# Nyström attention with a gated MLP on one core: later requests for q, k and v, the second group's scores behind the first group's transposes, and a pause behind each front

## The chip, the cores and the metric

The kernel runs on one core of a Trainium2 chip. The metric is the device time of one execution in microseconds, from the runs of the kernel; beside it stands one profiled execution, whose trace all rows come from. The engines are called as in the profile: PE multiplies matrices, PEld loads its weights, DVE is the vector engine, ACT the scalar engine, POOL the third elementwise engine, and SP issues all DMAs here. "Clock" is the share of its full clock that PE was granted.

## What is computed

```python
# q, k, v: (8 images, 8 heads, 576, 64) float32
q_lm = q.reshape(B, H, 32, S // 32, D).mean(axis=3)     # 32 landmarks
k_lm = k.reshape(B, H, 32, S // 32, D).mean(axis=3)
A, Bm, C = sm(q, k_lm), sm(q_lm, k_lm), sm(q_lm, k)     # softmax of scaled scores
Z = Bm.T / (norm1(Bm) * norminf(Bm) + 1e-6)
for _ in range(6):
    Z = 2 * Z - Z @ Bm @ Z
x = (A @ Z @ C @ v).transpose(0, 2, 1, 3).reshape(4608, 512)
xn = x / sqrt(mean(x * x) + 1e-6) * rms_g
out = (silu(xn @ w_gate) * (xn @ w_val)) @ w_out        # 512 -> 1536 -> 512
```

## The kernel before

Each image is taken in two groups of four heads, g = 0 and 1. Its attention part is a set of generators. `stage1(b, g)` sums q and k to landmarks (`lmT`, two DVE reductions), then multiplies the scores: this is called the **front** here, sixteen `sC`/`sA` multiplications for each 288 columns and one small one, into four PSUM banks of the pool `pa`, which has four banks in all. The maxima (`mx`), the exponentials `E` and `eb` (ACT) and the transposes `tA` (DVE) empty these banks. Its second half, `back()`, takes the softmax of A (`mA`, POOL's subtraction, ACT's exponential, `sumA`, POOL's product, `AT`), transposes `E` on PE (`sE`, `sF`) and multiplies with v (`pCV`). `newton(b)` runs the iteration (`p`, `pn`, `pW`, `pT`), `second(b)` multiplies the attention output's squares (`pO`, `sq`, `pss`, `pms`), and its end is a chain of small DVE steps `ms`, `r` and then `tA`, `af`, `an`: `an` is the normalized image that the MLP reads, for both groups.

The MLP takes the hidden width in two halves: first all eight images with the first half (`mlp(early, ...)`, chunk 0 to 7, partial sums written to memory), then all eight with the second (`mlp(late, ...)`). A chunk multiplies six tiles of the hidden width (`psg`, `psv` into four banks of the pool `pg`; ACT's Silu and DVE's product free them; `h`), then the outputs (`pso`). Weights are split into a high and a low part, and the gate and value weights are multiplied with the attention factor `WT` first (`pM`, then `Mhi` on ACT and `Mlo` on DVE, from the same `pg` banks). A weight tile is loaded (`fetch`), put together by one ACT and three DVE instructions (`load_next`), in the order of a list.

What orders the two is a `Mixer`: each MLP multiplication adds a planned time (`MMG`, `MMO`) to a clock, and after each one generator whose due time has come is run to its next `yield`. `yield a, w` says that the part takes a of planned PE time and may go on w after it (times `slack`); `yield -w` asks again after w. PE's multiplications keep this program order; other engines' orders come out of a scheduler that moves instructions by readiness and priority, so that the code alone does not show them. Requests for DMAs wait on SP's queue in order, for their buffer to come free too.

Of the kernel before, what the change touches and what calls it, by code (L numbers as in the profile page):

```python
# [12 lines left out]
AF = mybir.ActivationFunctionType  # L13
# [21 lines left out]
BW = 5.0  # L35
SW2 = 2.4
# [5 lines left out]
WW = 1.0  # L42
WAIT0 = 3.0
WAIT1 = 4.0
NPAIR = 3
NF1 = 2 * NPAIR


@with_exitstack
def nystrom_moe_kernel(  # L50
# [12 lines left out]
    nc = tc.nc  # L63
    w_gate, w_val, w_out = (w.bitcast(I32) for w in (w_gate, w_val, w_out))
    B, G = q.shape[:2]
# [55 lines left out]
    class Weights:  # L121
# [28 lines left out]
        def load_next(self):  # L150
            if not self.order:
                return
            f, nm = self.order.pop(0)
            while (f, nm) not in self.raws:
                self.fetch()
            raw, shp = self.raws.pop((f, nm))
            whead, wtail = raw[..., 1], raw[..., 0]
            if nm == "o":
                wf = mp.tile(shp, F32, name="w32", tag="w32", bufs=WB)
            else:  # L160
                pair = f // 2
                if pair not in self.gv:
                    self.gv[pair] = self.place("gv", pair), []
                at = (f % 2 * 2 + "gv".index(nm)) * P
                wf = self.gv[pair][0][:, :, at : at + P]
                self.gv[pair][1].append(nm)
            w = wf.bitcast(I32)
            with tc.issue_after(self.after) if self.after else nullcontext():
                nc.scalar.activation(wf, whead.bitcast(F32), AF.Copy, scale=2.0**-112)
            nc.vector.tensor_scalar(  # L170
                w, w, 3, 1, op0=ALU.logical_shift_left, op1=ALU.bitwise_or
            )
            nc.vector.scalar_tensor_tensor(
                w, whead, -0x80000000, w, op0=ALU.bitwise_and, op1=ALU.bitwise_or
            )
            nc.vector.scalar_tensor_tensor(
                w, wtail, 29, w, op0=ALU.logical_shift_right, op1=ALU.bitwise_or
            )
            if nm == "o":
                hi, lo = self.place("o", f)  # L180
                nc.scalar.copy(hi, wf)
                nc.gpsimd.tensor_sub(lo, wf, hi.bitcast(F32))  # L182
                self.out[f] = hi, lo
            while self.queue and len(self.raws) < self.ahead:
                self.fetch()
# [7 lines left out]
    class Mixer:  # L193

        def __init__(self):
            self.streams = []
            self.clock = 0.0
            self.slack = SLACK0

        def add(self, gen, urgent=False):  # L200
            self.streams.append([gen, 0.0, urgent])

        def part(self):
            for st in list(self.streams):
                if st[1] > self.clock:
                    continue
                with tc.high_priority() if st[2] and HP else nullcontext():
                    wait = next(st[0], None)
                if wait is None:
                    self.streams.remove(st)  # L210
                elif not isinstance(wait, tuple):
                    st[1] = self.clock - wait
                else:
                    self.clock += wait[0]
                    st[1] = self.clock + wait[1] * self.slack
                    return True
            return False
# [6 lines left out]
        def drain(self, done):  # L224
            while self.streams and not done():
                if not self.part() and self.streams:
                    self.clock = max(self.clock, min(st[1] for st in self.streams))

    mix = Mixer()

# [1 line left out]
        fs = range(f0, f0 + NF1)  # L232
        return [(f, nm) for f in fs for nm in "gv"] + [(f, "o") for f in fs]

    mixed, gated = {}, {}

    def mix_weights(wts, b, pair):

# [21 lines left out]
    def mlp(wts, b, f0, an, store, part, following):  # L260
# [4 lines left out]
        for n, pair in enumerate(pairs):  # L265
# [4 lines left out]
            for i in range(2):  # L270
                s = mp.tile([P, S], F32, name="s", tag="s", bufs=2)
                for e in range(2):
                    cols = slice(e * HS, (e + 1) * HS)
                    banks = []
                    for z in range(2):
                        ps = pg.tile([P, 512], F32, name=f"ps{'gv'[z]}", tag="pg")
                        at = slice((2 * i + z) * P, (2 * i + z + 1) * P)
                        for g in range(G):
                            for w, a in ((mhi, 0), (mhi, 1), (mlo, 0)):
                                mm(  # L280
                                    ps[:, :HS],
                                    w[:, g, at],
                                    an[:, a, g, cols],
                                    start=(g == 0 and w is mhi and a == 0),
                                    stop=(g == G - 1 and w is mlo),
                                )
                                yield MMG
                        banks.append(ps[:, :HS])
                    nc.scalar.activation(s[:, cols], banks[0], AF.Silu)  # L289
                    nc.vector.tensor_mul(s[:, cols], s[:, cols], banks[1])  # L290
                if len(hs) < NF1:
                    f = len(hs)
# [37 lines left out]
    with tc.tile_pool(name="ap", bufs=1, side="right") as ap, tc.tile_pool(  # L330
# [19 lines left out]
        def stage1(b, g):  # L350
# [5 lines left out]
            with tc.issue_after(gated[b - 2].ins) if b > 1 else nullcontext():  # L356
                for z in range(2):
# [3 lines left out]
                        axis=AX.X,  # L361
                        op=ALU.add,
                    )
            nxt = (b, 1) if g == 0 else (b + 1, 0)
            if b > 0 and nxt[0] < B:
                load_qk(*nxt)
                load_v(*nxt)
            yield 0.0, KW2
            while b and g and stage["second"] < 0:
                yield -0.3  # L370

            sC = [pa.tile([P, 512], F32, name="sC", tag="pa") for e in range(2)]
            sA = [pa.tile([P, 512], F32, name="sA", tag="pa") for e in range(2)]
# [11 lines left out]
            for h in range(4):  # L385
                mm(
                    psB[rows(rho(g, h)), :],
                    lmT[half(h), 0, h // 2, :],
                    lmT[half(h), 1, h // 2, :],
                    start=True,  # L390
                    stop=True,
                )
            sC = [s[:, :HS] for s in sC]
            sA = [s[:, :HS] for s in sA]
            mx = sm.tile([P, 3], F32, name="mx", tag="mx")
# [22 lines left out]
            for e in range(2):  # L418
# [1 line left out]
                    tA[:, e * (NB // 2) : (e + 1) * (NB // 2), :].rearrange("p n m -> p (n m)"),  # L420
                    sA[e],
                )
            yield 1.3, 0.0
            if g == 1:
                stage["front"] = b

            def back():
                yield -BW * mix.slack
                while b and stage["second"] < 0:
                    yield -0.3  # L430
                mA = sm.tile([P, NB], F32, name="mA", tag="mA")
# [19 lines left out]
                EL = ap.tile([2 * M, P], F32, name="EL", tag="EL", bufs=1)  # L451
                nc.scalar.copy(ET, sE)
                nc.scalar.copy(EL, sF)
                yield 0.65, SW2
                pCV = pa.tile([P, D], F32, name="pCV", tag="pa")
                for ch in range(5):
                    for h in range(4):
# [6 lines left out]
                            stop=(ch == 4),  # L464
                        )
                nc.vector.tensor_scalar_mul(nt["PV"][:, g, M:], pCV, rs[:, 0:1])
                yield 0.85, 0.2
                done[b] = done.get(b, 0) + 1
                if done[b] == 2:
# [158 lines left out]
        nc.sync.dma_start(gsb, rms_g.rearrange("(k p) -> p k", p=P))  # L628
        nc.gpsimd.tensor_scalar_mul(gsb, gsb, RS)

        stage = {"front": -1, "first": -1, "newton": -1, "second": -1, "chunk": -1, "outs": -1, "wt": -1}

        def firsts():
            for b in range(1, B):
# [27 lines left out]
        mix.add(stage1(0, 0))  # L662
        mix.add(stage1(0, 1))
        mix.drain(lambda: False)
        for _ in range(4):
            early.fetch()
        load_qk(1, 0)
        load_v(1, 0)
        for _ in range(4, NF1 + 2):
            early.fetch()  # L670
        early.ahead, early.after = 2, fixed["eb", 0, 0].ins
        mix.add(seconds(), True)
# [23 lines left out]
        def lates():  # L696
            while stage["first"] < B - 1:
# [5 lines left out]
            late.spots = itertools.cycle(  # L703
                [(lq, "lraw", 4), (mp, "wraw", 2), (lq, "lraw", 4)]
            )
            yield from late.stream(WAIT1, 5)
            while "rest" not in places:
                yield -0.3
# [4 lines left out]
        late = Weights(order, place_late, ring, 5)  # L713
# [76 lines left out]
```

## Time and profile before

| | us |
|---|---|
| median of 3 runs | 862.11 (861.26 to 862.2) |
| the profiled execution, whole | 866.44 |
| its span from first to last instruction | 864.6 |
| PE busy | 806.0 |
| DVE busy | 519.2 |
| ACT busy | 326.3 |
| mean clock granted to PE | 0.959 |

The profiled execution was 4.33 us longer than the median of the runs, and 1.84 us of it lie outside the span. Chunk 0 begins its `psg` multiplications in earnest at 63.1 us of the span, chunks 1 to 7 at 133.0, 197.0, 254.2, 318.7, 374.8, 438.9 and 485.8, and the second half of the width at 532.0 us. In rows of a timeline the columns are the start, the length, the engine, the line, the operation with what it writes and reads, and in brackets how long the engine was idle before and what it waited for. In rows of windows, each engine has its busy time and in brackets the number of instructions, then the granted clock and the DMAs' share.

### The profile page before, as it was taken

The page shows a single profiled execution, that of the slowest core. Times are in us where ns is not written, and L with a number is a line of the kernel's source. Part 1 is how long each engine was busy: PE and PEld are TensorE (multiplying, and loading weights), DVE is VectorE, ACT ScalarE, POOL GpSimd, SP SyncE. Part 2 cuts the span into 40 slices and gives each one's busy share as a digit, 9 for nine tenths or more (in the row PEclk, how much of TensorE's full clock was granted, in tenths as well). Part 3 has the DMA queues.
Part 4 walks back from the last instruction along what each step waited for, and adds up shares of the span by engine and source line. Part 5 has one row for each costly group of instructions (what it writes and reads, how often), then busy time and mean ns, then how long its engine had stood idle before and what let it go on. Part 6 is the DMA issues. An engine that isn't in the chain of part 4 may idle for free.

```text
span 864.6 us, 17425 instructions
## 1 busy us (share of the span) xinstructions
PE 806.0 (93%) x7190; PEld 635.9 (74%) x7190; DVE 519.2 (60%) x1131; ACT 326.3 (38%) x708; POOL 82.5 (10%) x109
## 2 busy tenths in 40 slices
PE   6548989989989999899899999999999999999998
PEld 3326757767768678678578697888888888878796
DVE  6998996674765855875975972443334242525341
ACT  3246445344354434343453653232223131404140
POOL 2012320020120110110201030000000000000000
PEclk7578999999989999999999999999999999999999
DMA  9654453151151250430262821123221323131202
GB/s 325 223 205 147 137 176 119 38 205 41 62 180 30 97 185 2 138 131 2 80 208 80 308 81 50 58 95 103 76 92 61 104 74 104 50 128 50 73 25 73
DMA packets 41054, 95.49 MB, mean 110 GB/s; under 512 B 4112, under 2 KB 17424, under 8 KB 38928
## 3 DMA queue, kind: packets, MB, share of 16 engines
q1 hardware_dynamic: 40976, 94.39, 32.0%
q8 instruction: 56, 0.92, 0.5%
q14 instruction: 22, 0.18, 0.1%
HBM read 66.06 MB, written 28.31 MB: 109 GB/s over the span
## 4 chain that ended last, share of the span: by engine, by line
PE 76%; DVE 17%; ACT 3%; DMA 3%; issue 1%; POOL 1%; SPq 0%; DVEq 0%; ACTq 0%; POOLq 0%
PE pso L104 27%; PE psg L104 19%; PE psv L104 18%; PE pM L104 4%; PE pn L104 2%; DVE lmT L358 2%; DVE Mlo L255 1%; PE pO L104 1%; PE pCV L104 1%; DVE mx L399 1%; DVE tA L419 1%; DVE tA L605 1%; DVE an L610 1%; DMA wrawv<-in_moe_w_val_dram 1%; DVE af L608 1%
## 5 line engine op out<-in xcount | busy, mean ns | idle before, releaser
L104 PE MATMUL pso<-whio,h 128*128 128x512 f32 x432 | 147.2, 413 | 2.2 <-ACT ob L683 2.2
L290 DVE TENSOR_TENSOR s<-s,psv 128x288 f32<-128x288 f32 x192 | 86.4, 450 | 85.8 <-PE psv L104 76.9
L104 PE MATMUL pso<-lhio,h 128*128 128x512 f32 x432 | 136.5, 392 | 0.0
L289 ACT ACTIVATE s<-psg 128x288 f32<-128x288 f32 x192 | 78.7, 412 | 99.2 <-PE psg L104 99.0
L298 DVE TENSOR_TENSOR h<-s,h 128x576 fp32r<-128x576 f32 x96 | 72.9, 760 | 56.5 <-ACT h L297 56.5
L104 PEld LDWEIGHTS pso<-whio,h 128*128 128x128 f32 x432 | 84.2, 197 | 26.1 <-ACT ob L683 4.9
L254 ACT CAST Mhi<-pM 128x512 fp32r<-128x512 f32 x96 | 51.5, 590 | 132.1 <-PE pM L104 131.9
L104 PEld LDWEIGHTS pso<-lhio,h 128*128 128x128 f32 x432 | 81.1, 188 | 22.5 <-DVE obl L742 5.9
L297 ACT CAST h<-s 128x576 fp32r<-128x576 f32 x96 | 64.6, 673 | 85.4 <-DVE s L290 85.4
L104 PE MATMUL psg<-an,Mhi 128*128 128x288 f32 x384 | 87.3, 310 | 6.0 <-ACT an L609 4.0
L104 PE MATMUL pso<-wloo,h 128*128 128x512 f32 x216 | 89.7, 415 | 0.5 <-POOL wloo L182 0.5
L742 DVE TENSOR_TENSOR obl<-obl,pso 128x512 f32<-128x512 f32 x36 | 24.6, 687 | 104.3 <-PE pso L104 104.3
L255 DVE TENSOR_TENSOR Mlo<-pM,Mhi 128x512 fp32r<-128x512 f32 x96 | 61.8, 681 | 41.4 <-ACT Mhi L254 41.4
L104 PE MATMUL psv<-an,Mhi 128*128 128x288 f32 x384 | 85.7, 305 | 0.0
L104 PE MATMUL pso<-lloo,h 128*128 128x512 f32 x216 | 84.1, 389 | 0.0
L104 PE MATMUL psg<-anl,Mhi 128*128 128x288 f32 x384 | 81.7, 301 | 0.6 <-DVE Mlo L255 0.6
L104 PE MATMUL psv<-anl,Mhi 128*128 128x288 f32 x384 | 79.1, 294 | 0.0
L104 PEld LDWEIGHTS psg<-an,Mhi 128*128 128x128 f32 x384 | 62.5, 191 | 16.6 <-ACT an L609 4.1
L104 PEld LDWEIGHTS psg<-anl,Mhi 128*128 128x128 f32 x384 | 61.0, 188 | 15.5 <-issue 12.6
L104 PEld LDWEIGHTS psv<-an,Mhi 128*128 128x128 f32 x384 | 63.0, 190 | 4.2 <-issue 2.4
L104 PEld LDWEIGHTS psv<-anl,Mhi 128*128 128x128 f32 x384 | 61.5, 188 | 0.0
L104 PE MATMUL psv<-an,Mlo 128*128 128x288 f32 x192 | 58.5, 304 | 0.0
(136 smaller groups left out, 1262.8 us busy)
## 6 DMA issues: line engine op xcount, KB each, us to landing
qk<-in_q_dram SPq DMA_DIRECT2D x16, 576.0 KB, 5.7
qk<-in_k_dram SPq DMA_DIRECT2D x16, 576.0 KB, 6.7
ad<-an SPq DMA_DIRECT2D x8, 1152.0 KB, 5.1
pd<-ob SPq DMA_DIRECT2D x36, 256.0 KB, 2.7
anl<-ad SPq DMA_DIRECT2D x8, 1152.0 KB, 5.1
obl<-pd SPq DMA_DIRECT2D x36, 256.0 KB, 2.7
out_dram<-obl SPq DMA_DIRECT2D x36, 256.0 KB, 2.0
vt<-in_v_dram SPq DMA_DIRECT2D x16, 512.0 KB, 4.1
```

What stands on the lines that cost most here:

```text
L104: tc.keep_in_program_order(nc.tensor.matmul(*args, **kw))
L254: nc.scalar.copy(hi[:, g], ps[g])
L255: nc.vector.tensor_sub(lo[:, g], ps[g], hi[:, g].bitcast(F32))
L289: nc.scalar.activation(s[:, cols], banks[0], AF.Silu)
L290: nc.vector.tensor_mul(s[:, cols], s[:, cols], banks[1])
L297: nc.scalar.copy(h[:, 0, TAIL:], s)
L298: gated[b] = nc.vector.tensor_sub(h[:, 1, TAIL:], s, h[:, 0, TAIL:].bitcast(F32))
L358: nc.vector.tensor_reduce(lmT[:, z], qk[z].rearrange("p h (m c) -> p h m c", c=LM), axis=AX.X, op=ALU.add,)
L399: nc.vector.tensor_reduce(mx[:, e : e + 1], sC[e], axis=AX.X, op=ALU.max)
L419: nc.vector.transpose(tA[:, e * (NB // 2) : (e + 1) * (NB // 2), :].rearrange("p n m -> p (n m)"), sA[e],)
L605: eng.tensor_mul(tAs[g], tAs[g], r1.unsqueeze(2).broadcast_to([P, NB, M]))
L742: nc.vector.tensor_add(ob, ob, ps)
```

## The change

It has these parts. `load_qk` and `load_v` for image b + 1 are asked for behind the last multiplication that reads the same group of image b (`sC`/`sA` for q and k, `pCV` for v), not at the start of `stage1`; at the beginning both groups of image 1 are asked for between the first weights. The front of group 1 waits until group 0's `ET` and `EL` are written (`stage["turned"]`) and one more us, where it followed group 0's front by its due time alone. Behind each front of images 1 to 7 the mixer runs no generator for 2.0 us of its clock (`QUIET`); the back of group 0 of image 1 loses its first pause. The second half's first five weight tiles are asked for ahead of their stream, and their first ACT step is ordered behind the last Silu issued so far.

```diff
@@ load_next
-            with tc.issue_after(self.after) if self.after else nullcontext():
+            after = self.after or silu.get("last")
+            with tc.issue_after(after) if after else nullcontext():
                 nc.scalar.activation(wf, whead.bitcast(F32), AF.Copy, scale=2.0**-112)
@@ Mixer.part
+            if self.clock < self.quiet:
+                return False
...
                     self.clock += wait[0]
+                    self.quiet = self.clock + sum(wait[2:])
@@ Mixer.drain
-                    self.clock = max(self.clock, min(st[1] for st in self.streams))
+                    self.clock = max(self.clock, self.quiet, min(st[1] for st in self.streams))
@@ mlp
-                    nc.scalar.activation(s[:, cols], banks[0], AF.Silu)
+                    silu["last"] = nc.scalar.activation(s[:, cols], banks[0], AF.Silu).ins
@@ stage1
-            nxt = (b, 1) if g == 0 else (b + 1, 0)
-            if b > 0 and nxt[0] < B:
-                load_qk(*nxt)
-                load_v(*nxt)
             yield 0.0, KW2
-            while b and g and stage["second"] < 0:
+            while b and g and stage["turned"] < b:
                 yield -0.3
+            if b and g:
+                yield 0.0, 1.0
...
+            if 0 < b < B - 1:
+                load_qk(b + 1, g)
...
-            yield 1.3, 0.0
+            yield 1.3, 0.0, QUIET * (b > 0)
@@ back
-                yield -BW * mix.slack
+                if (b, g) != (1, 0):
+                    yield -BW * mix.slack
...
-                yield 0.65, SW2
+                yield 0.65, 0.0
+                if g == 0:
+                    stage["turned"] = b
+                yield 0.0, SW2
...
                 nc.vector.tensor_scalar_mul(nt["PV"][:, g, M:], pCV, rs[:, 0:1])
+                if 0 < b < B - 1:
+                    load_v(b + 1, g)
@@ beginning
-        for _ in range(4):
-            early.fetch()
-        load_qk(1, 0)
-        load_v(1, 0)
-        for _ in range(4, NF1 + 2):
-            early.fetch()
+        for g in range(2):
+            for _ in range(4 - g * 2):
+                early.fetch()
+            load_qk(1, g)
+            load_v(1, g)
+        for _ in range(2):
+            early.fetch()
@@ lates
+            for _ in range(5):
+                late.fetch()
+            yield -WAIT1
             yield from late.stream(WAIT1, 5)
```

At the end of chunk 2 PE has, before the change, the front of group 1 of image 4 (its last row is `sC<-lmT`) and one output multiplication later the transposes of group 0:

```order
L104 MATMUL sA<-qk_2843,lmT 32x288
L104 MATMUL sC<-lmT 32x32 x4
L104 MATMUL pso<-whio_971,h_831 128x512
L107 MATMUL sE<-ident,E 128x128 x4
L107 MATMUL sF<-ident,E 64x128
L104 MATMUL pso<-wloo_972,h_831 128x512
```

and with the change the transposes stand ahead of it, five output multiplications and the `pM` of chunk 3 between them, and the front is followed by the first `psg` of chunk 3:

```order
L108 MATMUL sE<-ident,E 128x128 x4
L108 MATMUL sF<-ident,E 64x128
L105 MATMUL pso<-wloo_1215,h_1240 128x512
L105 MATMUL pso<-whio_1214,h_1240 128x512 x2
...
L105 MATMUL pM<-wgv_433,WT 32x512 x8
...
L105 MATMUL sA<-qk_2290,lmT 32x288
L105 MATMUL sC<-lmT 32x32 x4
L105 MATMUL psg<-an,Mhi 128x288 x2
L105 MATMUL psg<-an,Mlo 128x288
```

So the transposes no longer stand directly behind the front that fills all four banks; the front itself has moved to the chunk's boundary.

ACT, at the same boundary, before the change (the exponentials of group 1's front, `tA` of its back, then the copies and Silu of chunk 3):

```order
L405 ACTIVATE E,ss<-sC,mx 128x288 x2
L409 ACTIVATE eb,ss<-sC,mx 128x32
L434 ACTIVATE tA<-tA 128x576
L683 COPY ob<-pso 128x512 x2
L254 CAST Mhi<-pM 128x512 x2
L289 ACT_TABLE_LOAD
L289 ACTIVATE s<-psg 128x288 x2
```

and with the change:

```order
L260 CAST Mhi<-pM 128x512 x2
L295 ACT_TABLE_LOAD
L295 ACTIVATE s<-psg 128x288
L411 ACT_TABLE_LOAD
L411 ACTIVATE E,ss<-sC,mx 128x288 x2
L415 ACTIVATE eb,ss<-sC,mx 128x32
L295 ACT_TABLE_LOAD
L295 ACTIVATE s<-psg 128x288 x2
L441 ACT_TABLE_LOAD
L441 ACTIVATE tA<-tA 128x576
L303 CAST h_807<-s 128x576
```

The exponentials now stand between the Silus of chunk 3, with a table load at each switch (four more loads at this boundary, four at that of chunks 4 and 5, two in chunk 0: 26 in all, 16 before).

On PE, in chunk 3, the second half of `pO` of image 4 stood, before, among `psg` and `psv`:

```order
L104 MATMUL psv<-an,Mlo 128x288
L104 MATMUL pO<-AT,W 64x288 x8
L104 MATMUL psg<-an,Mhi 128x288 x2
L104 MATMUL psg<-an,Mlo 128x288
L104 MATMUL psv<-an,Mhi 128x288 x2
```

and now stands eight output multiplications and a `pM` behind the front of group 0 of image 5:

```order
L105 MATMUL sC<-lmT 32x32 x4
L105 MATMUL pso<-wloo_1157,h_1162 128x512
...
L105 MATMUL pM<-wgv_406,WT 32x512 x8
L105 MATMUL pO<-AT,W 64x288 x8
L105 MATMUL pso<-whio_932,h_807 128x512
...
L105 MATMUL pss<-sq,ones 32x288 x8
...
L108 MATMUL sE<-ident,E 128x128 x4
...
L105 MATMUL pms<-sqT,sel 128x18
```

With it `pss` and `pms` of the image that the next chunk reads have moved towards that chunk's start.

More of the change, by code (lines that the diff above doesn't have):

```diff
@@ L44 @@
 WAIT1 = 4.0
+QUIET = 2.0
 NPAIR = 3
@@ L197, in __init__ @@
             self.clock = 0.0
+            self.quiet = 0.0
             self.slack = SLACK0
@@ L233, in weight_order @@
         return [(f, nm) for f in fs for nm in "gv"] + [(f, "o") for f in fs]
-    mixed, gated = {}, {}
+    mixed, gated, silu = {}, {}, {}
     def mix_weights(wts, b, pair):
@@ L629, in nystrom_moe_kernel @@
         nc.gpsimd.tensor_scalar_mul(gsb, gsb, RS)
-        stage = {"front": -1, "first": -1, "newton": -1, "second": -1, "chunk": -1, "outs": -1, "wt": -1}
+        stage = {"front": -1, "first": -1, "newton": -1, "second": -1, "chunk": -1, "outs": -1, "wt": -1, "turned": -1}
         def firsts():
```

## Prediction

> **What bounds the kernel now.** I read the page's engine rows first, then the windows of the stages, then PE's waits, then the timeline at the longest of them.
>
> ```profile
> span 864.6 us, 17425 instructions
> PE 806.0 (93%) x7190; PEld 635.9 (74%) x7190; DVE 519.2 (60%) x1131; ACT 326.3 (38%) x708; POOL 82.5 (10%) x109
> ```
>
> ```profile
> 63.13:133.90 70.77, 61.59 (x683) 45.79 (x682) 65.21 (x146) 39.29 (x85) 21.41 (x21) 0.93 0.49 168
> 254.24:317.90 63.66, 60.51 (x665) 45.73 (x661) 41.61 (x101) 27.03 (x61) 6.26 (x5) 0.97 0.31 103
> 529.50:864.60 335.10, 330.57 (x2185) 278.09 (x2184) 130.44 (x228) 92.76 (x193) 7.12 (x24) 1.00 0.22 76
> ```
>
> PE carries the span. The windows (length, then PE, PEld, DVE, ACT, POOL, clock) are chunk 0, chunk 3 and the second half of the width. In chunk 0 DVE is busy 65.2 of 70.8 us and sets the pace with PE; in chunk 3 PE idles 3.2 us and DVE has room; behind 529.5 us the change reaches nothing. PE's waits from 130 to 500 us (total, times, longest):
>
> ```profile
> PE sE L107 <- DVE tA L419: 10.9, 5, 2.8
> PE psg L104 <- ACT s L289: 1.9, 1, 1.9
> PE sF L107 <- DVE sumA L437: 0.7, 2, 0.4
> PE sF L107 <- ACT ET L452: 0.7, 1, 0.7
> PE sF L107 <- DVE mx L402: 0.4, 1, 0.4
> ```
>
> `sE` waits once in each of chunks 1 to 5. The timeline at the one of chunk 3:
>
> ```profile
> 299.76 0.26 PE L104 MATMUL sC<-lmT 64*32 64x32 f32 x8
> 299.95 0.51 PE L104 MATMUL pso<-whio,h 128*128 128x512 f32 x1
> 302.36 0.45 DVE L399 TENSOR_REDUCE mx<-sC 128x1 f32<-128x288 f32 x1
> 302.72 0.47 DVE L419 STREAM_TRANSPOSE tA<-sA 128x288 f32<-128x288 f32 x1
> 303.25 0.66 PE L107 MATMUL sE<-ident,E 128*128 128x128 f32 x4 [2.79 <-DVE tA L419]
> ```
>
> Group 1's front has filled all four `pa` banks, and one multiplication later PE stands at `sE` until DVE, busy with `an` and `sumA` until then, has transposed a bank free. The granted clock drops behind each of the five; the windows of the third one, and the sum over all five:
>
> ```profile
> 304.76:308.17 3.41, 3.41 (x10) 2.62 (x9) 2.78 (x7) 1.83 (x8) 2.27 (x2) 0.50 0.91 309
> sum 20.48, PE 18.70 PEld 14.85 DVE 15.88 ACT 11.25 POOL 10.60; mean PE 3.74 PEld 2.97 DVE 3.18 ACT 2.25 POOL 2.12
> ```
>
> **What goes.** The transposes now stand ahead of group 1's front, so these five waits have lost their cause: 10.9 + 0.7 + 0.7 + 0.4 = 12.7 us. For the clock, the starts of output multiplications at full and at half:
>
> ```profile
> 237.10 0.63 PE L104 MATMUL pso<-whio,h 128*128 128x512 f32 x2
> 237.79 0.62 PE L104 MATMUL pso<-whio,h 128*128 128x512 f32 x2
> 245.62 1.05 PE L104 MATMUL pso<-whio,h 128*128 128x512 f32 x2
> 246.90 0.63 PE L104 MATMUL pso<-whio,h 128*128 128x512 f32 x1
> ```
>
> Three take 237.79 - 237.10 = 0.69 us, or 0.23 each; at half clock 1.28 us, or 0.43. Of the 18.70 us worked at half clock 46% is lost, 8.6 us. Together 21.3 us, if no wait takes their place.
>
> The Trainium skill ("TensorE: Matmul & The Clock Gate", Part 1) has the clock drop after at least one idle window of some 3.4 us. The trace disagrees: an idle of 2.79 us within 3.8 us brought 3.41 us at 0.50. By the page the new waits below would cost no clock at all, 1.6 us less than my sum.
>
> **What comes.** Two kinds of wait, both at boundaries of chunks.
>
> First, `an`. Between `pms` and the next chunk's first `psg` now stand, in PE's order, at the ends of chunks 2 and 4, 27 output multiplications, `sE` and `sF`, a `pM` and the front. The `pM` row is:
>
> ```profile
> 437.00 1.09 PE L104 MATMUL pM<-wgv,WT 64*32 64x512 f32 x16
> ```
>
> So 27 x 0.23 + 0.66 + 0.27 + 1.09 + 1.2 (front, an estimate from 16 pairs that end at 300.02 and begin about 298.8) = 9.4 us. At the ends of chunks 3 and 5 the same count gives 9.2 us, of chunk 0 7.6 us, of chunk 1 14 us. Before, this was 25 us and more (`pms` 288.47, chunk 4 from 318.7). DVE's chain from `pms` to the last `an`, undisturbed in chunk 6 and among a front's steps in chunk 3:
>
> ```profile
> 467.87 0.29 PE L104 MATMUL pms<-sqT,sel 128*128 128x18 f32 x2
> 475.86 0.76 DVE L610 TENSOR_TENSOR an<-af,an 128x576 fp32r<-128x576 f32 x1 [0.74 <-ACT an L609]
> 288.47 0.29 PE L104 MATMUL pms<-sqT,sel 128*128 128x18 f32 x2
> 300.29 0.75 DVE L610 TENSOR_TENSOR an<-af,an 128x576 fp32r<-128x576 f32 x1
> ```
>
> 8.5 us from `pms`' end, and 12.3 us. At the ends of chunks 2 and 4 DVE has two `Mlo`, `sumA` and `AT` between the steps, so I take 11.0; group 1's part of `an` is needed 0.5 us after the first `psg`, which leaves a wait of 1.1 us there (0 to 2.4). Chunks 3 and 5 have group 1's maxima in it but neither of these: 9.4 us, no wait (0 to 2.6). Chunk 0: 1.5 us (0 to 4.2). Chunk 1: none.
>
> Second, ACT. Table loads and their cost:
>
> ```profile
> L289 ACT ACT_TABLE_LOAD x8 | 10.3, 1283 | 1.2 <-PE psg L104 1.0
> L405 ACT ACT_TABLE_LOAD x6 | 7.7, 1283 | 22.4 <-DVE mx L402 22.3
> ```
>
> At the starts of chunks 3 and 5 the first Silus stand apart by two loads each time, and the exponentials wait for DVE's maxima in ACT's order. The four added loads take 5.1 us of ACT; the `pg` banks let PE run one half (about 1.8 us) ahead. Followed bank by bank this leaves PE waits of 0.8 and 1.8 us, 2.6 in all per start (0, if the banks cover it, to 5.1). At the starts of chunks 4 and 6, and of chunk 2, the exponentials come ahead of one load, and `Mhi` and Silu come late: 1.3, 1.3 and 0.8 us.
>
> In chunks 3 and 5 the second `pO` stands 8 x 0.23 + 1.09 = 2.9 us behind group 0's front and needs its banks. The front's chain in chunk 3 of before:
>
> ```profile
> 291.22 0.46 DVE L399 TENSOR_REDUCE mx<-sC 128x1 f32<-128x288 f32 x1
> 294.06 0.15 DVE L402 TENSOR_TENSOR mx<-mx,nscale 128x2 f32<-128x2 f32 x1
> 294.14 1.28 ACT L405 ACT_TABLE_LOAD   x1
> 295.44 0.50 ACT L405 ACTIVATE E<-sC,mx 128x288 f32<-128x288 f32 x1
> ```
>
> The first maximum starts about its own length ahead of the front's end, so the factor (294.21) is there 2.5 us behind that end; ACT's load, 1.28 us, then held the exponentials, of 0.5 us each. Without it the second bank is free at about 3.6 us, a wait of 0.7 in each of the two chunks (2.0 with the load as here).
>
> Sum: 1.1 x 2 + 1.5 + 2.6 x 2 + 1.3 x 2 + 0.8 + 0.7 x 2 = 13.7 us. Such short waits can leave the clock alone, as one of 1.91 us in chunk 7 (its row is below) did:
>
> ```profile
> 485.77:529.50 43.73, 41.82 (x266) 36.31 (x263) 27.74 (x48) 19.34 (x38) 6.79 (x5) 1.00 0.42 151
> ```
>
> For one of the two long boundaries I add a slow window, 3.41 x 0.46 = 1.6: 15.3 us.
>
> **The rest.** In chunk 0, before, DVE put together a weight of the second half in the middle of its busiest stretch:
>
> ```profile
> 109.98 0.41 DVE L170 TENSOR_SCALAR w<-w 128x512 int32<-128x512 int32 x1
> 110.43 0.69 DVE L173 SCALAR_TENSOR_TENSOR w<-wrawo,w 128x512 int32<-128x512 int32 x1
> 111.16 0.69 DVE L176 SCALAR_TENSOR_TENSOR w<-wrawo,w 128x512 int32<-128x512 int32 x1
> ```
>
> Its first step is now tied to a Silu, so 1.8 us leave chunk 0, and group 1's `sumA` and `AT` leave it too. I take 2.0 us (0, if PE's order binds, to 4). The one wait on ACT of chunk 7:
>
> ```profile
> 487.53 0.67 ACT L169 ACTIVATE lgv<-wrawv 128x512 f32<-128x512 f32 x1 [1.45 <-DMA wrawv<-in_moe_w_val_dram]
> 489.53 0.53 PE L104 MATMUL psg<-an,Mhi 128*128 128x288 f32 x2 [1.91 <-ACT s L289]
> ```
>
> A late weight held ACT ahead of `Mhi` and Silu. Five weights are now asked for earlier, and their first step goes behind a Silu: 1.9 us go (0 if the loads still come late). The requests for q, k and v:
>
> ```profile
> qk<-in_q_dram SPq DMA_DIRECT2D x16, 576.0 KB, 5.7
> ```
>
> They land within 5.7 us and are needed a chunk (57 to 64 us) later: nothing, though the writes of `ob` and `an` stand in other places behind them on SP; if that cover is gone, a late `qk` holds `lmT` and a front for 5.7 us. The pause adds no instruction; what it delays is `second`, priced above as late `pms`.
>
> In all -21.3 + 15.3 - 2.0 - 1.9 = -9.9 us. The profiled execution took 866.44 us (864.6 span and 1.84 around), so 856.5; it stood 4.33 above the median of 862.11, which gives 852.2.
>
> **Rivals.** (1) The waits move by less: if the banks cover ACT's loads and DVE's chain is near 8.5 us, half of the 15.3 stays, and the time is 844.5. For it speak DVE's 41.6 busy of 63.7 us in chunk 3; against it the in-order ACT at the boundary.
>
> (2) Slower: `an` decides. If its chain takes 12.3 us behind each late `pms`, PE waits 12.3 - 7.6 at chunk 0's end and 2.4, 2.6, 2.4, 2.6 at the next ones, 14.7 us, and each is long enough for a slow window, 5 x 1.6; with 10.0 of ACT's and `pO`'s waits this is 32.7 for 15.3: 869.6. It decides from 25.2 us of new waits on, 5 a boundary.
>
> (3) No change: the new waits just make up 25.2 us, 862.
>
> (4) ACT's order at the two starts costs all that it can: eight added loads of 1.28 us, none covered, are 10.3 us in place of 5.2, and each start gets a slow window, 3.2 us for 1.6: 858.9. Against it speak the `pg` banks, one half ahead.
>
> The Trainium skill ("ScalarE: Activation LUTs", What ACT_TABLE_LOAD costs) speaks harder against the change: a load of about 1.28 us and a drain of some 1.38 at every switch, by which 8 x 2.66 = 21.3 us in place of 5.2 would give 868. The first part agrees with the rows; of the drain they show nothing, since the exponential begins 0.02 us behind its load.
>
> **Numbers.** My forecast 0.45 (its own range 847 to 858), (1) 0.18, (2) 0.20, (3) 0.10, (4) 0.07. The range, 842 to 867, leaves out the worse half of (2) and the case of (1) in which hardly a wait stays. 0.2% (1.7 us) is about what a measurement can tell from no change: faster 0.70 (the forecast, (1) and (4)), same 0.10, slower 0.20.
>
> **What would show it.** `sE <- tA` gone from PE's waits and the clock at 1.00 through chunks 1 to 5: right. New rows `psg <- ACT s` or `psg <- DVE an` at 254, 319, 375 and 439 us less the gain, above 5 us each with slow windows: wrong, rival (2). `pO <- ACT eb` above 2 us: the front's chain was underrated. Chunk 0 no shorter than 70 us: PE's order binds there.

## The result, and the profile after

The changed kernel takes 875.61 us (median of 4 runs, 874.31 to 875.95) against 862.15 for the kernel before in the same session (861.26 to 864.56): ratio 1.0149, 95% interval 1.0126 to 1.0172. It is 13.5 us slower; 852.2 was forecast, with a range that ended at 867. The page's first rows:

```profile
span 873.7 us, 17413 instructions
PE 810.6 (93%) x7190; PEld 638.6 (73%) x7190; DVE 516.3 (59%) x1131; ACT 337.5 (39%) x718; POOL 85.8 (10%) x109
```

The same 7190 multiplications keep PE busy 4.6 us longer, and ACT has ten instructions more, all table loads. Where the time lies is seen in windows from chunk start to chunk start (length; busy time of PE, PEld, DVE, ACT, POOL; clock). Before, chunk 0 and chunks 1 to 7:

```profile
56.50:132.97 76.47, 62.23 (x681) 46.10 (x681) 70.94 (x159) 40.22 (x87) 21.41 (x21) 0.89 0.49 168
132.97:531.99 399.02, 382.12 (x3883) 293.35 (x3875) 270.94 (x630) 175.95 (x385) 46.51 (x50) 0.97 0.32 108
```

and after:

```profile
57.55:138.95 81.40, 65.89 (x695) 47.45 (x695) 63.42 (x145) 39.56 (x82) 18.63 (x19) 0.86 0.46 150
138.95:540.99 402.04, 383.01 (x3904) 295.01 (x3896) 274.91 (x643) 187.03 (x398) 51.03 (x52) 0.98 0.33 111
```

The work ahead of chunk 0 grew by 1.0 us, chunk 0 by 4.9, chunks 1 to 7, which were to gain, by 3.0; the second half of the width is equal to 0.1 us. The trace of before is long for its kernel, though, by 4.3 us. Against the trace of e3 below, whose PE has the same work in the same order and whose two stretches take 75.24 and 394.73 us, chunk 0 grew by 6.2 us and chunks 1 to 7 by 7.3. Note DVE in chunk 0: it worked 71 of 76 us before and only 63 of 81 after. The stretch has become longer and DVE idler, so something else holds it.

**Chunks 1 to 7.** PE's waits after, from 130 to 500 us:

```profile
PE psg L105 <- DVE Mlo L261: 10.4, 4, 2.8
PE psg L105 <- ACT s L295: 4.3, 4, 1.7
PE psg L105 <- DVE an L622: 0.8, 2, 0.4
```

The rows of `sE` and `sF`, 12.7 us together, are gone, and 15.5 us stand in their place. The largest, at the start of chunk 4, on ACT, DVE and PE:

```profile
321.24 1.08 ACT L260 CAST Mhi<-pM 128x512 fp32r<-128x512 f32 x2
322.41 0.26 DVE L511 STREAM_TRANSPOSE nsbt<-nsb 128x128 f32<-128x128 f32 x1
323.83 0.78 DVE L449 STREAM_TRANSPOSE AT<-tA 128x576 f32<-128x576 f32 x1
324.57 0.68 DVE L261 TENSOR_TENSOR Mlo<-pM,Mhi 128x512 fp32r<-128x512 f32 x1
325.24 0.67 DVE L261 TENSOR_TENSOR Mlo<-pM,Mhi 128x512 fp32r<-128x512 f32 x1
325.30 0.54 PE L105 MATMUL psg<-an,Mhi 128*128 128x288 f32 x2 [2.85 <-DVE Mlo L261]
```

`Mhi` is written at 322.3, but on DVE two chains of short steps come ahead of `Mlo`: the start of Newton's iteration (`nsum` to `nden`) and group 1's `sumA` to `AT`. The first output bank of `pM` is thus released at 325.2, and PE stands. In the kernel before neither chain stood ahead of `Mlo` at this boundary, and it was DVE that waited there:

```profile
318.63 1.29 DVE L255 TENSOR_TENSOR Mlo<-pM,Mhi 128x512 fp32r<-128x512 f32 x2 [3.69 <-ACT Mhi L254]
```

So DVE's steps behind a front are the same as ever, and PE waits for them at another place.

A smaller one hides in PE's busy time. In chunk 3 the second `pO` behind group 0's front:

```profile
298.85 1.28 ACT L411 ACT_TABLE_LOAD   x1
299.84 0.71 PE L105 MATMUL pO<-AT,W 32*64 32x288 f32 x8
300.63 0.49 ACT L411 ACTIVATE E<-sC,mx 128x288 f32<-128x288 f32 x1
300.79 1.46 PE L105 MATMUL pO<-AT,W 32*64 32x288 f32 x8 [0.24 <-ACT E L411]
```

The sixteen rows end 2.4 us after they begin, where 0.74 us is usual; only 0.24 us is shown as a wait, since the second bank's wait lies inside the row of 1.46. Chunks 3 and 5 lose 1.7 us each, and chunk 0 2.2.

**Chunk 0.** DVE after, at its start, with group 0's back of image 1 (`mA`, `sumA`, `AT`) and the first steps of the next weights:

```profile
52.73 0.74 DVE L439 TENSOR_REDUCE mA<-tA 128x18 f32<-128x576 f32 x1
56.52 0.73 DVE L443 TENSOR_REDUCE sumA<-tA 128x18 f32<-128x576 f32 x1
61.64 0.77 DVE L449 STREAM_TRANSPOSE AT<-tA 128x576 f32<-128x576 f32 x1
62.97 0.68 DVE L175 SCALAR_TENSOR_TENSOR wgv<-wrawg,wgv 128x512 int32<-128x512 int32 x1
```

Before, the same weight step stood ahead of the back:

```profile
56.25 0.67 DVE L173 SCALAR_TENSOR_TENSOR wgv<-wrawg,wgv 128x512 int32<-128x512 int32 x1
62.39 0.71 DVE L432 TENSOR_REDUCE mA<-tA 128x18 f32<-128x576 f32 x1
```

6.7 us later on DVE: the steps of the back take 2.6 us of it, and two `Mlo` and the end of `an`, which stood behind the weight before, most of the rest. That is not caught up, since the last step on a raw weight frees the buffer that the next request waits for. SP's requests after, in this place (start, length, what):

```profile
64.88 0.38 SPq L148 DMA_DIRECT2D wrawg<-in_moe_w_gate_dram  x1
67.14 0.33 SPq L347 DMA_DIRECT2D qk<-in_q_dram  x1
70.90 0.54 SPq L148 DMA_DIRECT2D wrawv<-in_moe_w_val_dram  x1
```

Before, the two weights were asked for at 58.26 and 67.65. PE, after:

```profile
80.24 1.96 PE L105 MATMUL pM<-wgv,WT 64*32 64x512 f32 x16 [7.95 <-DVE wgv L178]
87.63 0.61 PE L105 MATMUL psg<-an,Mhi 128*128 128x288 f32 x1 [3.10 <-DVE Mlo L261]
```

The second `pM` waits 8.0 us (3.92 before), and the next `psg` another 3.1, for ACT, which copies `Mhi` only when the following weight has landed. The clock is at half for longer: 0.86 over the chunk, 0.89 before.

These waits are not the whole of the 4.9 us. Before, PE had a wait in chunk 0 of the kind that the change removes:

```profile
62.18 1.09 PE L107 MATMUL sE<-ident,E 128*128 128x128 f32 x4 [5.07 <-DVE mx L402]
```

It is gone after, so that PE's idle time in chunk 0 grew only from 14.2 to 15.5 us. The other 3.7 us lie in PE's busy time: 15.7 us were worked at half clock for 10.7 before, the second `pO` hides 1.0 of its 2.2, and the 40 multiplications of group 1's front, done ahead of chunk 0 before (from 51.3 us, where PE then still waited 3.95 for `an`), now stand in it at 65.4.

### The profile page after: what moved, and what is told of

It reads as the page before. It is cut to its first block, busy times and chain, and to the rows that moved or that the text cites. A ratio compares the mean times of both kernels' runs of the same rounds, so it can differ in the third digit from the quotient of the medians.

```text
span 873.7 us, 17413 instructions
## 1 busy us (share of the span) xinstructions
PE 810.6 (93%) x7190; PEld 638.6 (73%) x7190; DVE 516.3 (59%) x1131; ACT 337.5 (39%) x718; POOL 85.8 (10%) x109
## 4 chain that ended last, share of the span: by engine, by line
PE 71%; DVE 17%; ACT 7%; issue 2%; DMA 2%; POOL 1%; SPq 0%; DVEq 0%; ACTq 0%; POOLq 0%
PE pso L105 26%; PE psg L105 17%; PE psv L105 16%; PE pM L105 3%; PE pn L105 2%; PE pO L105 1%; DVE Mlo L261 1%; DVE an L622 1%; DMA qk<-in_q_dram 1%; ACT E L411 1%; DVE af L620 1%; ACT L411 1%; PE sC L105 1%; DVE lmT L364 1%; DVE sumA L443 1%
## 5 line engine op out<-in xcount | busy, mean ns | idle before, releaser
L105 PE MATMUL pso<-whio,h 128*128 128x512 f32 x432 | 142.2, 400 | 0.9 <-DVE h L304 0.9
L105 PE MATMUL psg<-an,Mhi 128*128 128x288 f32 x384 | 93.0, 324 | 25.8 <-DVE Mlo L261 13.5
L105 PEld LDWEIGHTS pso<-whio,h 128*128 128x128 f32 x432 | 80.1, 188 | 24.9 <-issue 6.2
L105 PEld LDWEIGHTS psg<-an,Mhi 128*128 128x128 f32 x384 | 65.5, 200 | 43.2 <-DVE Mlo L261 14.6
L105 PE MATMUL psv<-an,Mhi 128*128 128x288 f32 x384 | 89.2, 314 | 0.5 <-DVE Mlo L261 0.4
L105 PE MATMUL pso<-wloo,h 128*128 128x512 f32 x216 | 86.0, 398 | 0.0
L105 PEld LDWEIGHTS psg<-anl,Mhi 128*128 128x128 f32 x384 | 61.0, 188 | 15.5 <-issue 12.6
L105 PEld LDWEIGHTS psv<-an,Mhi 128*128 128x128 f32 x384 | 65.2, 197 | 5.0 <-DVE Mlo L261 0.9
L105 PE MATMUL psg<-an,Mlo 128*128 128x288 f32 x192 | 60.4, 314 | 0.0
```

What stands on the lines that cost most here:

```text
L105: tc.keep_in_program_order(nc.tensor.matmul(*args, **kw))
```

## The experiments

Each edit is against the kernel named in its diff's first line. "Chunk 0" is the length from its first `psg` to that of chunk 1; ratios are to the kernel before, on the same chip. Lengths of stages come from one trace each, and two traces of one order of work, before and e3, differ by 1.2 us in chunk 0 and by 4.3 in chunks 1 to 7.

### The parts alone

**e1**, the turn alone:

```diff
 # kernel before
-            while b and g and stage["second"] < 0:
+            while b and g and stage["turned"] < b:
                 yield -0.3
+            if b and g:
+                yield 0.0, 1.0
...
-                yield 0.65, SW2
+                yield 0.65, 0.0
+                if g == 0:
+                    stage["turned"] = b
+                yield 0.0, SW2
```

> The kernel before with one part of the change alone: group 1's front waits until group 0's ET and EL are written, and one us more; requests, pause, weights as before. Theory A (the turn is a gain, the pause and what it moves to the chunk boundaries is the loss): the five waits on tA (12.7 us) and most of the half-clock loss behind them (8.6 us) go, with under 6 us of new waits: 842 to 852 us. Theory B (the turn itself makes the second half of the attention late, whatever the pause does; the boundary waits on Mlo and Silu, 14.7 us in the changed kernel, are its price): those waits are there too, 858 to 868 us. Theory C (the loss sits in the beginning, where weights come late): as A, since the beginning is as before.

872.36 us, ratio 1.0109 (1.0059 to 1.0158). No theory foresaw it. PE's waits from 130 to 500 us:

```profile
PE pCV L104 <- DVE tA L421: 10.8, 6, 2.1
PE psg L104 <- DVE Mlo L255: 3.7, 3, 1.8
```

Without the pause `pCV` of group 0 stands one multiplication behind group 1's front, needs one of the four `pa` banks and waits for DVE's `tA` as `sE` did: 10.8 us for 12.7. And chunk 0 is 84.2 us long.

**e2**, the pause alone (`QUIET`, as in the change, on the kernel before):

> The kernel before with the pause of 2.0 us of the mixer's clock behind each front alone. Theory A: the transposes still stand behind group 1's front, so the five waits on tA stay or shrink a little, and the pause moves later parts towards the boundaries: 862 to 870 us, with new psg waits on Mlo or Silu. Theories B and C: the pause alone does nothing that can be measured, 860 to 864 us.

874.91 us, ratio 1.0137 (1.0091 to 1.0182), above all that was expected. Chunk 0 is 81.2 us: the pause alone moves group 1's front of image 1 into it, to 63.2 us, with group 0's transposes still behind that front, at 67.0. Later the wait is `sF` for `mx`, 8.3 us in 5.

**e3**, the requests for q, k and v alone (those of `stage1`, `back` and the beginning):

> The kernel before with the requests for q, k and v alone moved: behind the last use, and at the beginning both groups of image 1 between the first weights. Theory C (late weights at the beginning): the pM of the first pair that waited 3.9 us now waits 6 us or more, and the whole is 866 to 870 us. Theories A and B: the transfers stay hidden, 861 to 864 us.

862.84 us, ratio 1.0007 (0.9978 to 1.0036): no change, chunk 0 75.2 us. On their own the requests are hidden; Theory C falls.

**e4**, the change without its pause:

```diff
 # changed kernel
-QUIET = 2.0
+QUIET = 0.0
```

> The changed kernel with the pause set to 0. Theory A: group 1's fronts leave the chunk boundaries, the psg waits on Mlo (10.4 us from 130 us on) and Silu (4.3) fall below 5 us together and the second pO no longer waits for the exponentials: 855 to 862 us, the rest of the loss being the beginning's. Theory B: the waits stay, 872 to 877 us. Theory C: the beginning is hardly touched by the pause, 868 to 874 us.

866.01 us, ratio 1.0026 (0.9999 to 1.0054), between the ranges of A and C. Mlo's and Silu's waits fall to 2.4 and 0.5 us, but `pCV`'s are 10.2, and chunk 0 is 80.8. Its chunks 1 to 7:

```profile
138.14:531.54 393.40, 377.00 (x3903) 290.51 (x3895) 272.28 (x642) 177.17 (x389) 48.98 (x52) 0.99 0.33 112
```

With the same multiplications on PE they took 402.04 in the changed kernel. The pause thus costs 8.6 us there and hardly anything in chunk 0 (0.6), and the whole is 9.6 us shorter without it. What the four have in common: each one that moves group 1's front of image 1 into chunk 0 (e1, e2 and e4) has a chunk 0 of 81 to 84 us.

### Is it chunk 0?

**e5**, the change, with image 1 in the order of before:

```diff
 # changed kernel
-            while b and g and stage["turned"] < b:
+            while b and g and stage["second" if b == 1 else "turned"] < b - (b == 1):
                 yield -0.3
-            if b and g:
+            if b > 1 and g:
...
-            yield 1.3, 0.0, QUIET * (b > 0)
+            yield 1.3, 0.0, QUIET * (b > 1)
...
-                if (b, g) != (1, 0):
-                    yield -BW * mix.slack
+                yield -BW * mix.slack
```

> The changed kernel, but image 1 (whose attention lies in chunk 0) keeps the order of before: group 1's front ahead of group 0's transposes, no pause, the first pause of group 0's back restored. Theory D (a loss of its own sits in chunk 0, 81.4 us long against 75.2 to 76.5, because group 0's back now enters DVE ahead of the second pair's weights): chunk 0 is 75 to 77 us and the whole 868 to 872 us. Rival E (chunk 0 only hands its work on: what it saves there the later chunks lose): 874 to 877 us.

858.19 us, ratio 0.9944 (0.9921 to 0.9967): 17.4 us less than the changed kernel, and faster than before. Its windows of chunk 0 and of chunks 1 to 7:

```profile
56.69:125.08 68.39, 58.28 (x619) 43.43 (x620) 61.26 (x138) 37.16 (x76) 18.89 (x19) 0.91 0.46 152
125.08:524.79 399.71, 383.15 (x3943) 292.22 (x3935) 277.86 (x651) 179.50 (x395) 51.03 (x52) 0.99 0.34 114
```

Chunk 0 lost 13.0 us, but it also has 76 multiplications fewer, above all the 40 of group 1's front, again ahead of it, and 40 of a `pCV`, now in a later chunk. Chunks 1 to 7 nevertheless lost 2.3 us with 39 more in them, so that the work was not merely handed on: Rival E falls, Theory D holds, and is larger than expected. The boundary waits on `Mlo` and at `pO` are still there; those on Silu fell from 4.3 to 0.5, with 16 table loads as before for 26:

```profile
PE psg L105 <- DVE Mlo L261: 10.4, 6, 2.1
PE pO L105 <- ACT E L411: 3.4, 3, 1.1
```

**e6**, the pause behind group 1's fronts only (`QUIET * (b > 0) * g` in the changed kernel):

> The changed kernel with the pause behind group 1's fronts only, so that the front of group 1 is ten output multiplications and more ahead of the chunk's end and pCV nine behind the front. Theory F (the boundary waits come of the pause behind group 0's front, which pushes group 1's front to the boundary and the second pO behind a front; the waits of pCV without a pause come of its place one multiplication behind the front): psg waits on Mlo and Silu under 4 us from 130 us on (14.7 in the changed kernel), pCV's under 1 (9 without a pause), 858 to 864 us, the rest being chunk 0's. Rival G (a pause anywhere costs): 870 to 876 us.

873.96 us, ratio 1.014 (1.0111 to 1.017). Theory F falls. `pCV` waits only 0.6 us, as expected, but `psg` and `psv` wait for `Mlo` 10.1 us and for ACT's `ob` 3.7, and chunk 0 is 84.5.

**e7**, e5 and e6 together (`QUIET * (b > 1) * g` in e5):

> The two last edits together: image 1 as before, and the pause behind group 1's fronts only. Theories D and F: 850 to 857 us, faster than before. If only F holds, 858 to 864; if only D, 868 to 872.

861.95 us, ratio 0.9981 (0.9961 to 1.0001), 12.0 below e6 by image 1's order alone; chunk 0 is 71.6. Against e5 it gained nothing. It lies in the range given for F alone, but e6 has shown F false: the ranges did not foresee how much image 1's order is worth.

**e8**, the kernel before with e3's requests, and from image 2 on group 1's front behind group 0's `pCV`:

```diff
 # kernel before, with e3's edit
-            while b and g and stage["second"] < 0:
+            while b and g and stage["second" if b == 1 else "turned"] < b - (b == 1):
                 yield -0.3
...
+                if g == 0:
+                    stage["turned"] = b
                 yield 0.85, 0.2
```

> The kernel before with the requests moved, and from image 2 on group 1's front behind group 0's pCV (not only behind its transposes), without a pause: no part that needs a pa bank stands directly behind a front. Theory F (a part that needs a pa bank within a few multiplications of a front waits for DVE; nothing else is lost): no waits of sE, sF or pCV, 850 to 857 us. Rival H (the front stands 5 to 8 output multiplications ahead of the boundary in chunks 2 and 4, and near there its steps hold Mlo and Silu): psg waits of 2 us and more at these boundaries, 860 to 868 us.

859.77 us, ratio 0.9971 (0.9946 to 0.9995). `sE`, `sF` and `pCV` wait no more, and 5.4 us of `Mlo`, 3.2 of `ob` (of `psg` and `psv`) and 1.6 of `sA` for `PV` stand there instead: Rival H, nearly. PE idles 12.9 us in chunks 1 to 7 (16.9 before), and the clock falls in none of its windows from 82 us to 840; but this trace lies 2.3 us below the kernel's median.

### What holds chunk 0

**e9**, a third raw buffer, the order of PE's 7190 multiplications unchanged:

```diff
 # changed kernel
-        ring = itertools.repeat((mp, "wraw", 2))
+        ring = itertools.repeat((mp, "wraw", 3))
...
-        early.ahead, early.after = 2, fixed["eb", 0, 0].ins
+        early.ahead, early.after = 3, fixed["eb", 0, 0].ins
...
-                [(lq, "lraw", 4), (mp, "wraw", 2), (lq, "lraw", 4)]
+                [(lq, "lraw", 4), (mp, "wraw", 3), (lq, "lraw", 4)]
...
-TAB = 5
-ATB = 5
+TAB = 4
+ATB = 4
```

> The changed kernel with a third buffer for raw weight tiles (three may be asked for ahead); the room comes from one buffer less of tA and of AT. PE's order is that of the changed kernel. Theory K (chunk 0 is paced by a chain from weight to weight: DVE's last step on one tile frees its buffer, then request, landing, ACT, DVE; the back of group 0, now ahead on DVE, sits in that chain): the second pair's pM waits under 4 us (8.0 in the changed kernel), chunk 0 falls from 81.4 to 72 to 77 us, the whole is 864 to 871 us. Rival L (DVE's work or PE's order alone sets chunk 0): 79 to 83 us, 873 to 878 us.

869.61 us, ratio 1.0075 (1.0045 to 1.0104), 6.0 below the changed kernel. Chunk 0 and the second `pM`:

```profile
57.37:132.86 75.49, 64.59 (x694) 45.92 (x694) 63.67 (x145) 38.66 (x81) 20.00 (x19) 0.89 0.47 161
77.93 1.96 PE L105 MATMUL pM<-wgv,WT 64*32 64x512 f32 x16 [5.58 <-DVE nden L519]
```

Chunk 0 falls by 5.9 us, and the wait of 3.1 us behind the `pM` falls to 0.3, with the same multiplications in the same order and the same work on DVE. So a chain of requests did hold it in the changed kernel: Theory K. The `pM`'s own wait only fell to 5.6, not below 4, and ends with a step of Newton's start on DVE (`nden`).

**e10**, the turn for image 1 alone:

```diff
 # kernel before, with e1's edit to back()
-            while b and g and stage["second"] < 0:
+            while b and g and stage["second"] < 0 or b == 1 and g and stage["turned"] < b:
                 yield -0.3
+            if b == 1 and g:
+                yield 0.0, 1.0
```

> The kernel before with the turn for image 1 alone: only there group 1's front waits for group 0's transposes, and one us. Theory D (the loss is chunk 0's): chunk 0 is 80 to 85 us against 75.2 to 76.5, later chunks as before, 869 to 874 us, as much as the turn for all images cost. Rival M (the loss of the turn is spread over all chunks): 863 to 866 us.

869.37 us, ratio 1.0082 (1.0052 to 1.0111). Chunk 0:

```profile
55.90:139.25 83.35, 69.01 (x720) 49.98 (x720) 70.60 (x164) 43.72 (x87) 22.23 (x21) 0.84 0.47 155
```

One image's order, in one chunk, costs 7 us, and of PE's work only the 40 multiplications of group 1's front have changed stage, from ahead of chunk 0 into it. The second `pM` waits 6.0 us there. But it begins 20.7 us behind the chunk's start, 19.9 before, both its weights were asked for no later than before (57.6 and 63.4 us for 58.3 and 67.6), and PE's idle time in chunk 0 is the same, 14.3 us for 14.2. The loss lies behind this `pM` and in PE's busy time, with 18.1 us worked at half clock for 10.7. The late requests of the changed kernel are thus not the cause here.

**e13**, the requests back where they were, in the changed kernel (e3 undone):

> The changed kernel with the requests for q, k and v where they were before (at the start of stage1, and at the beginning only group 0 of image 1 between the weights). PE's order is that of the changed kernel. Theory N (the requests stand ahead of the second pair's value weight on SP and share its transfer: 3.3 us of its lateness): the wait at the second pM falls from 8.0 to about 5 us and the whole to 870 to 873 us. Rival O (the requests are hidden): 874.5 to 877 us.

874.75 us, ratio 1.0123 (1.009 to 1.0156). The wait at the `pM` falls by 1.2 us only (6.8), the time by 0.9, which is within the intervals. Theory N is mostly wrong: what delays the second weight is less the requests on SP than the step on DVE that frees its buffer.

**e14**, the first pause of group 0's back restored (`yield -BW * mix.slack` without its condition, in the changed kernel):

> The changed kernel with the first pause of group 0's back in image 1 restored; its transposes then stand 19 multiplications into chunk 0, still ahead of group 1's front. Theory P (the lost pause put the back's DVE steps ahead of the weights'): the wait at the second pM falls below 5 us, 868 to 871 us. Rival Q (the turn does it, wherever the back starts): 873 to 877 us, with a wait of 6 us or more.

872.73 us, ratio 1.0101 (1.0063 to 1.0139). The `pM` waits 5.5 us, less than the 6.0 with the turn alone, but then the first `psg` of chunk 1 waits 7.2 for `an`, and chunk 0 is 86.8: between the two theories.

### Faster ones

**e11**, e5 with the third buffer of e9:

> The changed kernel with image 1's order of before (the kernel of 858 us), and a third buffer for raw weights, with one buffer less of tA and AT. Theory K: chunk 0 falls below 68.4 us, by up to the 3.9 us that its second pM waits, 853 to 857 us. Rival L: the same chunk 0, 857 to 860 us.

856.55 us, ratio 0.9935 (0.9913 to 0.9958). Chunk 0 is 67.2 for 68.4, and its second `pM` still waits 4.0: with the weights' steps early on DVE the third buffer has little left to do.

**e12**, e8's order with the changed kernel's late weights (fetched ahead, first step behind the last Silu):

> The kernel with group 1's front behind pCV from image 2 on, no pause, image 1 as before, and with it the changed kernel's late weights (asked for ahead, first step behind the last Silu). If the late weights' three DVE steps, out of chunk 0, are what shortened it there: chunk 0 is 69 to 72 us (74.9 without), and the whole 853 to 858 us. If it was the pause that shortened it (parts moved into the next chunk): 74 to 76 us, 858 to 861 us.

856.37 us, ratio 0.9924 (0.9897 to 0.9951), with e11 the fastest. Chunk 0 is 72.4 for e8's 74.9: the late weights' DVE steps out of it are worth some 2.5 us, by one trace of each.

**e15**, e12 with the third buffer:

> The fastest kernel so far (group 1's front behind pCV from image 2 on, late weights, image 1 as before) with the third weight buffer, and one buffer less of tA and AT. If the chain of weights still paces its chunk 0 (its second pM waits 3.4 us): 853 to 855.5 us. If not, as without it, 855.5 to 858 us.

857.16 us, ratio 0.9921 (0.9893 to 0.9948): the same as e12. The two do not add up.

## Why the prediction was wrong

Forecast were -9.9 us on the profiled execution; from profile to profile the span grew 9.1. Step by step:

- **The five waits go**: right. 12.7 us of `sE` and `sF` are gone.
- **New waits at the boundaries**, 13.7 us without the clock: the kind was right, the owner partly wrong. `an` was 0.8 us at the boundaries and none at chunk 0's end (forecast 2.2 and 1.5); ACT's order 4.3 (5.2); the second `pO` 1.7 in chunks 3 and 5 (0.7), because the table load that I took for gone was there. The late `Mhi` and Silu at the starts of chunks 2, 4 and 6, 3.4 in the sum, became `Mlo`, 10.4, with a wait of 1.85 us at chunk 1 too. This is one step that failed: I followed ACT's copy and let DVE's `Mlo` come right behind it; DVE's steps of the back and of Newton's start move to this place with the front, and I did not lay them in DVE's row. Together 18.9 for 13.7: these waits alone exceed those that went. The pause brought them, where the prediction let it delay `second` alone. Without it, in e4, `pCV` waits 10.2 us instead, and chunks 1 to 7 are still 8.6 us shorter, by the clock in part (6.8 us worked at half for 12.9).
- **Chunk 0**, -2.0: this is the step that failed most, with 4.9 us the other way. I read DVE's 92% as "DVE sets the pace" and subtracted what left DVE. What came in was not costed: the 40 multiplications of group 1's front, more time at half clock, and group 0's back ahead of the weights on DVE. The window that I read began at 63.13 us, just behind the wait of 5.07 at `sE` that the turn removes, so that the steps not costed are worth more than the 4.9 us show. The subtracted part fits e12's 2.5. The sign named for a mistake here, a chunk 0 no shorter than 70 us, came true, but not its reading that PE's order binds: e9 took 5.9 us off with the same order.
- **The clock**, -8.6 and +1.6: in the trace before, 18.7 us were worked at half clock behind 130 us, after it 12.86, by this row, the sum of the four windows:

```profile
sum 13.65, PE 12.86 PEld 12.65 DVE 6.77 ACT 3.57 POOL 0.27; mean PE 3.21 PEld 3.16 DVE 1.69 ACT 0.89 POOL 0.07
```

  So 5.8 us of work, or 2.7 us of time by the same 46%, came back where 7.0 were counted on: four of the new waits of 1.7 to 2.85 us brought a slow window each.
- **Chunk 7**, -1.9: 0.5 the other way, by its length (46.7 us for 46.2). The wait for Silu is 0.45 instead of 1.91, but 0.94 for `h` has come at the outputs.
- **From the profile to the median**, -4.33: wrong in kind. The excess of the profiled execution was carried over as if the changed kernel had it too; its profile lies at its median. The excess is the clock's: e3's trace has the same waits as before and three slow windows behind 130 us where the trace of before has six, 10.2 us for 20.5. The forecast took these windows off twice, in the 8.6 and in the 4.33.

Added up, the steps miss by 5.2 (waits), 6.9 (chunk 0), 4.3 (clock), 2.4 (chunk 7) and 4.3 (median); with 1.0 us ahead of chunk 0 and 1.0 of `pCV`'s short waits, that is 25.1 for the 23.4 between 852.2 and 875.6, since waits of before on `ob` went as well.

Of the rivals, (2) had the sign, but its mechanism, `an`, made only 0.8 us of wait at the boundaries. The table loads of (4), and the drain that the Trainium skill adds to them ("ScalarE: Activation LUTs", What ACT_TABLE_LOAD costs), did not decide either: e6 has 18 loads where the changed kernel has 26, and is only 1.7 us faster.

What the runs do not settle: why chunk 0 is longer in every order with group 1's front of image 1 inside it. In the eight of these with two raw buffers (the changed kernel, e1, e2, e4, e6, e10, e13, e14) it takes 80.8 to 86.8 us, and in all eight kernels with that front ahead of it 67.2 to 76.5; the turn alone (e10) and the pause alone (e2) are each enough. In the changed kernel e9 shows that the chain of raw buffers carries 5.9 us. In e1, e2, e10 and e14 the weights are asked for as early as before, so that something else, of the clock in part, must hold there. Nor does a run take e5 without any pause, which cost 8.6 us with the other order of image 1.

## What to carry to other kernels

When four banks and one in-order engine stand behind a stretch of work, moving the waiting instruction need not remove the wait: PE stood at `sE`, or at `pCV`, or for `Mlo`, 10 to 13 us in all. Ask which steps must be done, and where nobody waits for them.

A high busy share does not make an engine the bound. In chunk 0 a chain ran through it (last step on a weight, buffer free, request, landing, ACT, DVE), and steps put ahead of a link delay all that follows, though the engine's total work stays the same. Look at what each link waits for before subtracting work.

A gain in one part can hide behind a loss in another: nearly all of the change was kept in e5, and it was faster than before. And a window that begins behind a wait hides what its removal will do. Reading each stage's length first would have shown it at once.

## What the runs showed of the hardware

The granted clock is set in steps of 3.41 us, at places that shift against the program from run to run, and PE's idle time within one step mostly decides the next. The same wait of 2.25 us before `sE` in chunk 2 fell differently in two traces. In the trace of before, one step has 1.51 us of idle time, and half clock follows:

```profile
239.91:243.32 3.41, 1.90 (x40) 0.75 (x24) 3.23 (x9) 2.20 (x7) 0.00 (x0) 1.00 0.65 253
243.32:246.73 3.41, 2.67 (x9) 2.34 (x10) 2.57 (x10) 1.51 (x6) 1.00 (x1) 0.50 0.93 301
```

and in e3's, more evenly split over two steps, of 0.97 and 1.30 us idle, the clock stayed:

```profile
238.33:241.74 3.41, 2.44 (x42) 1.04 (x41) 2.77 (x8) 2.74 (x8) 0.00 (x0) 1.00 0.43 178
241.74:245.15 3.41, 2.11 (x12) 1.85 (x13) 3.13 (x11) 1.16 (x4) 0.44 (x1) 1.00 1.00 305
245.15:248.56 3.41, 3.41 (x52) 2.52 (x51) 1.43 (x4) 1.50 (x7) 1.84 (x2) 1.00 0.55 218
```

Over the 17 traces, from 46 to 840 us, counted from PE's records and the clock's steps:

| idle in a step | steps at full clock, and followed by half |
|---|---|
| under 1.0 us | 1 of 3578 |
| 1.0 to 1.5 us | 6 of 68 |
| 1.5 to 2.0 us | 34 of 60 |
| 2.0 us and more | 54 of 54 |

The way back is harder: of steps at half clock 91 of 94 with under 0.4 us of idle time were followed by full, 4 of 23 with 0.4 to 1.0, none of 46 with more. This fits chunk 0, where PE waits in many steps and the clock stays at half for 3.4 to 17 us once it has fallen. The Trainium skill ("TensorE: Matmul & The Clock Gate", Part 1) has the drop behind a whole idle window; here 2.0 us within a step of 3.41 were enough every time, and 1.5 to 2.0 in 34 of 60 cases, so that the position of the wait counts. This goes with the scatter of one kernel's times (858.31 to 869.33 in 29 runs of the kernel before), and a wait of 1.5 to 3 us costs its length and, by where it falls, some 1.6 us more (an estimate: one step of 3.41 us times the 46%).
